# Block-sparse attention feeding an FFN: from the seventh tile on, the scores of both halves in one block and their values in another, and the fourth head in the free column group

## The chip, the cores and the metric

One core of one Trainium2 chip. The time is device microseconds of one execution of the whole program. The median over several runs is compared; the profile describes one execution.

## The reference, cut to what matters

```python
# attention: 4 batches, 8 heads, 768 tokens, head dim 64, blocks of 32 tokens (24 blocks)
scores = scale * q @ k.transpose(0, 1, 3, 2)
mask   = |qblock - kblock| <= 1, or either block is the first or the last (0, 23),
         or kblock is one of 3 blocks drawn for this qblock
attn   = exp(where(mask, scores, -1e9) - max); attn /= attn.sum(-1) + 1e-9
x      = (attn @ v).transpose(0, 2, 1, 3).reshape(3072, 512)
# FFN
h   = maximum(x @ w_in, 0)            # w_in 512 x 2048
out = (h * h) @ w_out                 # w_out 2048 x 512, all fp32
```

A query block therefore sees 8 key blocks: three of the window, the first and the last, and three drawn ones. The query blocks 0 and 23 see all 24.

## The kernel before

**Tiles and halves.** The 3072 tokens are 24 tiles of 128, listed in `order` as (b, t), batch 0 to 3 and t 0 to 5; tile number k counts from 0. A tile has four query blocks (*groups*), except t = 0 and t = 5, which have three: their first or last query block sees all keys and is done apart. Attention of a tile is done in two *halves* u of four heads each (`class Half`). Scores (`s`) go to two PSUM banks per half, by 32-column groups of TensorE, one group for each query block: window keys straight from `kn`, the keys of the whole half and batch; first, last and drawn keys from `KG`, a gathered tile. `static_keys` copies the first and last key block out of `kn` into `KG`, on ACT, for the first two tiles of each batch (there are two `KG`). DVE then takes maxima and subtracts them (`m`, `p`), ACT takes 16 small exponentials (`pm`, four for each group, 12 with three groups), DVE transposes 32 x 32 blocks (`pT`), TensorE multiplies with the values (`pv`, 65 columns a head: 64 and the sum), and DVE divides (`norm`, into `x`). Tiles 0 to 5 use another form (`exps`, `turn` by TensorE, `copies`), since `MOVED = 6`.

**Global blocks.** The query blocks 0 and 23 of a batch make four units of a head pair (`class Whole`): scores `g`, exponentials `pg`, moves `pgm`, transpose `pTg`, values `pvg`.

**FFN.** Eight chunks c of three tiles. A chunk has 16 blocks f of 128 hidden units. For each, 12 matmuls make the hidden block `ph` (line 800); ACT takes its ReLU `r` and the square `gh`; DVE takes `gf` from `ph` and `r` (line 816); POOL takes the rest `gl`; nine matmuls, two blocks later, add to the output `po` (line 838). Weights are cut in two parts on DVE and POOL (`wi`, `wo`), and in chunk 0 are also prepared by ACT from raw loads (`craw`). Chunk 0 multiplies plain fp32 (`gp`, line 828). `xt`, `xh`, `xl` turn and split x at a chunk's start; `ot` copies the output.

**The order of work** is written by hand: engines take instructions in the order of the program. The FFN of a chunk yields 96 times (*pieces*; 83 us for a chunk without global blocks, 0.86 each), and after each piece a `Stream` resumes the attention units of the chunk ahead whose time has come. A unit's own `yield n` is a lag in pieces. From chunk 2's tiles on, a half starts every 16 pieces: scores, 4 pieces, 16 exponentials with a piece between each, 11 pieces, values. So the values of a half come directly before the scores of the half two places on, in one block. The four wholes of a batch start 9 pieces behind its first four halves.

**Memory that both share.** The tag `s` has five PSUM banks, taken in turn by scores, `ph`, `pv`, `g`, `pvg`, `xt` and `pt`. The three output accumulators have their own three. Each batch's `kn` of a half is one buffer; in chunk 0 it is loaded on POOL's queue, later on SP's.

## Time and profile before

| | |
|---|---|
| median of 3 runs | 755.57 us (752.95 to 756.13) |
| profiled execution, its own time | 753.14 us |
| its span | 751.4 us |
| mean granted TensorE clock | 0.997 |
| instructions | 24184 |
| moved by DMA | 92.95 MB, 124 GB/s on the mean |

Attention of the first three tiles alone fills the first 57 us. FFN chunk 0 runs from about 57 to 153 us; from there a chunk takes 83 or 92 us, depending on whether a batch's global blocks fall into it, and the last has no attention beside it (675 to 752 us). A row of the page gives an engine's busy time; a timeline row gives a start, a length, the engine, the line, the operation with the tile written and read, and in brackets the idle time before it with what ended it. Matmul lengths overlap, so steps from start to start are what TensorE spends.

### The profile page before, as it was taken

To read this page: it belongs to the slowest core of one execution; us is meant where nothing else is said; L and a number is where in the kernel's file an instruction comes from. 1 tells how busy PE (TensorE), PEld (TensorE's weight loads), DVE (VectorE), ACT (ScalarE), POOL (GpSimd) and SP (SyncE) were. 2 spreads that over 40 slices of the span, in tenths; PEclk is the share of its full clock that TensorE was granted. 3 is DMA by queue.
4 is the path that set the end of the run, shared out by engine and by line. 5 is a ranking of instruction groups with operands and counts; after the bars stand their busy time and mean duration, and the time that the engine had idled before them with its cause. 6 is when DMAs were issued, how large, how long until landed. Compare 5 with 4: busy or idle time off the path is not lost.

```text
span 751.4 us, 24184 instructions
## 1 busy us (share of the span) xinstructions
PE 726.4 (97%) x8936; PEld 608.1 (81%) x8936; DVE 497.4 (66%) x988; ACT 518.8 (69%) x1145; POOL 500.4 (67%) x624
## 2 busy tenths in 40 slices
PE   5779999999999999999999999999999999999997
PEld 2566766678888888888888888888888888898986
DVE  5786786757786756667876665667868666545452
ACT  5997778888876866588786777578876776623222
POOL 6963643337776675767777567666867576777885
PEclk9999999999999999999999999999999999999999
DMA  8785889552533435543533435634344342101001
GB/s 276 226 231 151 261 251 344 132 156 56 144 90 92 136 85 173 150 99 101 148 72 100 132 89 177 161 85 123 93 120 102 89 129 52 34 1 43 1 1 42
DMA packets 85786, 92.95 MB, mean 124 GB/s; under 512 B 13539, under 2 KB 73060, under 8 KB 85668
## 3 DMA queue, kind: packets, MB, share of 16 engines
q1 hardware_dynamic: 79684, 68.42, 34.6%
q0 software_dynamic: 5696, 22.58, 9.2%
q8 instruction: 71, 1.16, 0.7%
q14 instruction: 47, 0.39, 0.2%
q10 hardware_dynamic: 288, 0.39, 0.1%
HBM read 85.05 MB, written 6.29 MB: 122 GB/s over the span
## 4 chain that ended last, share of the span: by engine, by line
PE 87%; ACT 6%; DVE 2%; DMA 2%; issue 1%; SPq 1%; ACTq 0%; POOL 0%; DVEq 0%; POOLq 0%
PE ph L800 34%; PE po L838 30%; PE s L373 6%; PE pv L470 6%; PE po L828 4%; PE g L558 2%; PE pvg L616 2%; DMA V<-in_v_dram 1%; PE xt L785 1%; ACT pm L418 1%; ACT V L217 1%; ACT V L209 1%; DMA kn<-in_kn_dram 1%; PE pt L447 1%; ACT p L432 1%
## 5 line engine op out<-in xcount | busy, mean ns | idle before, releaser
L800 PE MATMUL ph<-xh,wi 128*128 128x384 f32 x832 | 237.8, 346 | 0.0
L418 ACT ACTIVATE pm<-p 32x256 f32<-32x256 f32 x528 | 219.2, 415 | 15.7 <-DVE p L393 8.2
L838 PE MATMUL po<-wo,gh 128*128 128x512 f32 x672 | 213.8, 399 | 0.0
L767 POOL TENSOR_TENSOR wi<-W,wi 128x512 fp32r<-128x512 f32 x104 | 143.4, 1379 | 68.6 <-DVE wi L766 34.7
L804 ACT ACTIVATE r<-ph 128x384 f32<-128x384 f32 x128 | 63.1, 493 | 174.9 <-PE ph L800 174.0
L818 POOL TENSOR_TENSOR gl<-gf,gh 128x384 fp32r<-128x384 f32 x112 | 117.7, 1051 | 90.7 <-DVE gf L816 79.4
L767 POOL TENSOR_TENSOR wo<-WO,wo 128x512 fp32r<-128x512 f32 x112 | 146.2, 1306 | 47.4 <-DVE wo L766 46.5
L816 DVE SCALAR_TENSOR_TENSOR gf<-ph,r 128x384 f32<-128x384 f32 x112 | 62.3, 556 | 152.5 <-ACT r L804 139.9
L800 PEld LDWEIGHTS ph<-xh,wi 128*128 128x128 f32 x832 | 150.4, 188 | 13.1 <-issue 7.4
L838 PEld LDWEIGHTS po<-wo,gh 128*128 128x128 f32 x672 | 123.5, 188 | 22.8 <-issue 2.8
L800 PE MATMUL ph<-xl,wi 128*128 128x384 f32 x416 | 141.4, 340 | 0.0
L838 PE MATMUL po<-wo,gl 128*128 128x512 f32 x336 | 133.2, 397 | 0.0
L800 PEld LDWEIGHTS ph<-xl,wi 128*128 128x128 f32 x416 | 78.2, 188 | 7.0 <-issue 2.9
L766 DVE CAST wo<-WO 128x512 fp32r<-128x512 f32 x112 | 82.8, 739 | 0.0
L838 PEld LDWEIGHTS po<-wo,gl 128*128 128x128 f32 x336 | 63.1, 188 | 15.9 <-POOL gl L818 1.1
L385 DVE TENSOR_REDUCE m<-s 128x2 f32<-128x512 f32 (+1 forms) x96 | 61.5, 682 | 8.3 <-PE s L373 8.0
L811 ACT ACTIVATE gh<-r 128x384 fp32r<-128x384 f32 x112 | 59.0, 527 | 9.3 <-POOL wo L767 0.4
L470 PEld LDWEIGHTS pv<-V,pT 128*32 128x32 f32 x2816 | 46.8, 109 | 22.3 <-issue 11.0
L470 PE MATMUL pv<-V,pT 128*32 128x65 f32 x2816 | 55.1, 221 | 7.7 <-ACT pT L457 4.9
L800 PE MATMUL ph<-xh,WI 128*128 128x384 f32 x192 | 54.3, 344 | 0.8 <-ACT xh L788 0.8
L373 PE MATMUL s<-KG,q 64*32 64x160 f32 x1408 | 48.3, 301 | 0.7 <-ACT KG L288 0.7
L766 DVE CAST wi<-W 128x512 fp32r<-128x512 f32 x91 | 47.6, 523 | 0.0
(89 smaller groups left out, 918.7 us busy)
## 6 DMA issues: line engine op xcount, KB each, us to landing
craw<-in_w_dram POOLq DMA_DIRECT2D x32, 512.0 KB, 5.5
V<-in_v_dram SPq DMA_DIRECT2D x462, 32.5 KB, 1.9
KG<-in_k_dram SPq DMA_DIRECT2D x198, 64.0 KB, 1.9
V<-in_v_dram SPq DMA_DIRECT2D x28, 390.0 KB, 4.7
q<-in_q_dram SPq DMA_DIRECT2D x24, 256.0 KB, 2.8
out_dram<-ot SPq DMA_DIRECT2D x22, 256.0 KB, 3.9
V<-in_v_dram SPq DMA_DIRECT2D x16, 292.5 KB, 4.4
vn<-in_vn_dram SPq DMA_DIRECT2D x5, 780.0 KB, 5.6
```

The lines of the kernel that those rows point to most:

```text
L373: nc.tensor.matmul(self.sb[e][g * BLK : (g + 1) * BLK, i * NSLOT + a : i * NSLOT + z], q[r, j, pr, :], k, start=True, stop=True,)
L385: nc.vector.tensor_reduce(m[at, e], self.sb[e][at].rearrange("p (i c) -> p i c", i=2), axis=AX, op=ALU.max)
L418: nc.scalar.activation(p[a * BLK : (a + 1) * BLK, g], x[g * BLK : (g + 1) * BLK, :, a], AF.Exp, scale=SCALE)
L470: nc.tensor.matmul(po[g * BLK : (g + 1) * BLK, h * VW : (h + 1) * VW], self.pT[:, g, 2 * e + i, c], v[:, self.u, j, hv : hv + VW], start=( ...
L766: nc.vector.tensor_copy(w[:, 0], src)
L767: nc.gpsimd.tensor_tensor(w[:, 1], src, w[:, 0], op=ALU.subtract)
L800: nc.tensor.matmul(ph[:, :TOK], w, x, start=(i == 0), stop=(i == len(steps) - 1))
L804: nc.scalar.activation(r, ph[:, :TOK], AF.Relu)
L811: nc.scalar.activation(gh, r, AF.Square)
L816: nc.vector.scalar_tensor_tensor(gf, ph[:, :TOK], 0.0, r, op0=ALU.max, op1=ALU.mult)
L818: nc.gpsimd.tensor_tensor(gl, gf, gh, op=ALU.subtract)
L838: nc.tensor.matmul(acc[c][u], g[:, at], w[:, k], start=(f == 0 and i == 0), stop=(f == NF - 1 and i == 2))
```

## The change

From tile 6 on, two halves become a `Pair`, started every 32 pieces. Both halves' scores (four banks) are issued in one block. The maxima of half 0 follow at once, those of half 1 two pieces later. The exponentials of both halves are spread over the pieces 3 to 30, each half's transpose one piece after its last. The static keys for the next tile are copied at pieces 22 and 25. Both halves' values come in one block at piece 38, six pieces into the next pair. The first pair (tile 6, that is (1, 0)) copies the static keys of half 1 itself and then yields four pieces before its scores; those of half 0 are copied by tile 5.

In `values`, a tile with three groups used three of four column groups for each of four heads. Now the three groups of the first three heads take three column groups, and the fourth column group takes the fourth head, one group in each head's turn; `norm` then has three more small products, which put the fourth head's rows in place. This holds for all tiles.

The wholes get a table of their own for the start and for the values; their transposed tile is split in two halves that use another buffer tag.

The diff, without the parts that only carry the split of the whole's transposed tile through `copies` and `values`:

```diff
@@ -61,12 +61,17 @@
 PIECES = 96
-STEP = PIECES // (2 * UC)
+STEP = PIECES // UC
 EARLY = 23
+VALUES_AT = 38
+EXPS_AT = (3, 30)
+SECOND = 2
+KEYS_AT = 22
+BEFORE = 4
 LAST = 4
 LAG = {"s": 0, "e": 4, "v": 11, "x": 4, "t": 4, "c": 0, "v0": 13, "w0": 4, "w": 16, "n": -1}
-G_AT = 9
+WHOLES = ((9, 44), (25, 60), (41, 76), (57, 92))
 STEP_0 = 5
 STEP_1, FIRST_1 = 12, 0
@@ -335,20 +340,16 @@
             self.loads(0)
             yield lag["s"]
             self.maxima()
-            if self.moved:
-                yield lag["e"]
-                yield from self.turn_blocks()
-                yield lag["v"]
-            else:
-                yield lag["x"]
-                self.exps()
-                self.next_keys()
-                yield lag["t"]
-                pt = self.turn(bank)
-                yield lag["c"]
-                self.copies(pt)
-                self.loads(1)
-                yield lag["v0"]
+            yield lag["x"]
+            self.exps()
+            if self.u == 1:
+                self.next_keys(0)
+            yield lag["t"]
+            pt = self.turn(bank)
+            yield lag["c"]
+            self.copies(pt)
+            self.loads(1)
+            yield lag["v0"]
             po = self.values(bank)
             if lag["n"] >= 0:
                 yield lag["n"]
@@ -397,32 +398,30 @@
                     op=ALU.subtract,
                 )
-        def next_keys(self):
-
-            b, t = order[min(self.k + self.u, len(order) - 1)]
+        def next_keys(self, u):
+
+            b, t = order[min(self.k + 1, len(order) - 1)]
             if b > 0 and t < 2:
-                static_keys(b, t, 1 - self.u)
-
-        def turn_blocks(self):
+                static_keys(b, t, u)
+
+        def exps_of_blocks(self):
             x = self.p.rearrange("p h c a s -> p (h c) a s")
-            p = rot.tile([P, NJ, 8, BLK], F32, tag="p", name=f"pm{self.name}", bufs=PBUFS)
-            for g in range(NJ):
-                if g == 2:
-                    self.next_keys()
-                if g >= len(self.js):
-                    yield NJ
-                    continue
+            self.pm = rot.tile([P, NJ, 8, BLK], F32, tag="p", name=f"pm{self.name}", bufs=PBUFS)
+            for g in range(len(self.js)):
                 for a in range(NJ):
                     nc.scalar.activation(
-                        p[a * BLK : (a + 1) * BLK, g], x[g * BLK : (g + 1) * BLK, :, a], AF.Exp, scale=SCALE
+                        self.pm[a * BLK : (a + 1) * BLK, g], x[g * BLK : (g + 1) * BLK, :, a], AF.Exp, scale=SCALE
                     )
-                    yield 1
+                    yield
+
+        def turn_blocks(self):
+
+            n = len(self.js)
             self.pT = rot.tile([P, NJ, 4, 2, BLK], F32, tag="pT", name=f"pT{self.name}", bufs=2)
-            n = len(self.js)
             nc.vector.transpose(
-                self.pT[:, :n].rearrange("p j h c q -> p (j h c q)"), p[:, :n].rearrange("p j x s -> p (j x s)")
+                self.pT[:, :n].rearrange("p j h c q -> p (j h c q)"), self.pm[:, :n].rearrange("p j x s -> p (j x s)")
             )
         def exps(self):
@@ -460,35 +459,39 @@
         def values(self, bank):
             po = bank(f"pv{self.name}")
-            for i in range(2):
-                for e in range(2):
-                    h = 2 * i + e
-                    hv = h * VW
-                    for c in range(2):
-                        v = values_of(self.k)[c]
-                        for g, j in enumerate(self.js):
-                            nc.tensor.matmul(
-                                po[g * BLK : (g + 1) * BLK, h * VW : (h + 1) * VW],
-                                self.pT[:, g, 2 * e + i, c],
-                                v[:, self.u, j, hv : hv + VW],
-                                start=(c == 0),
-                                stop=(c == 1),
-                            )
+            n = len(self.js)
+            for h in range(n):
+                for c in range(2):
+                    v = values_of(self.k)[c]
+                    for g in range(NJ):
+                        src, of = (g, h) if g < n else (h, n)
+                        i, e = divmod(of, 2)
+                        j, hv = self.js[src], of * VW
+                        nc.tensor.matmul(
+                            po[g * BLK : (g + 1) * BLK, h * VW : (h + 1) * VW],
+                            self.pT[:, src, 2 * e + i, c],
+                            v[:, self.u, j, hv : hv + VW],
+                            start=(c == 0),
+                            stop=(c == 1),
+                        )
             return po
         def norm(self, po):
             t, u = self.t, self.u
             x = x_tile(self.b, t)
-            po3 = po[:, : HW // 2].rearrange("p (h c) -> p h c", h=H // 2)
+            n = len(self.js)
+            po3 = po[:, : n * VW].rearrange("p (h c) -> p h c", h=n)
             x3 = x[:, u * H // 2 * D : (u + 1) * H // 2 * D].rearrange("p (h c) -> p h c", h=H // 2)
-            rec = rot.tile([P, H // 2], F32, tag="rec", name=f"rec{self.name}", bufs=2)
-            at = self.rows
-            nc.vector.tensor_scalar(rec[at], po3[at, :, D], EPS, None, op0=ALU.add)
-            nc.vector.reciprocal(rec[at], rec[at])
-            rec3 = rec.unsqueeze(2).broadcast_to([P, H // 2, D])
-            parts = ((2 * BLK, 0, 2 * BLK), (BLK, 2 * BLK, 3 * BLK)) if t == 0 else ((0, 0, at.stop),)
+            rec = rot.tile([P, n], F32, tag="rec", name=f"rec{self.name}", bufs=2)
+            nc.vector.tensor_scalar(rec, po3[:, :, D], EPS, None, op0=ALU.add)
+            nc.vector.reciprocal(rec, rec)
+            rec3 = rec.unsqueeze(2).broadcast_to([P, n, D])
+            parts = ((2 * BLK, 0, 2 * BLK), (BLK, 2 * BLK, 3 * BLK)) if t == 0 else ((0, 0, n * BLK),)
             for to, a, z in parts:
-                nc.vector.tensor_tensor(x3[to : to + z - a], po3[a:z, :, 0:D], rec3[a:z], op=ALU.mult)
+                nc.vector.tensor_tensor(x3[to : to + z - a, :n], po3[a:z, :, 0:D], rec3[a:z], op=ALU.mult)
+            for g, j in enumerate(self.js if n < NJ else ()):
+                at = slice(n * BLK, P)
+                nc.vector.tensor_tensor(x3[j * BLK : (j + 1) * BLK, n], po3[at, g, 0:D], rec3[at, g], op=ALU.mult)
         def loads(self, step):
@@ -516,13 +519,55 @@
                 load_window(n, self.u)
                 load_sampled(n, self.u, nc.sync, SP)
+    class Pair:
+
+
+        def __init__(self, b, t):
+            self.halves = [Half(b, t, u) for u in range(2)]
+            self.b, self.t = b, t
+            self.first = order.index((b, t)) == MOVED
+
+        def events(self):
+
+            first, second = self.halves
+            ev = [(0, first.maxima), (SECOND, second.maxima)]
+            ev += [(KEYS_AT, lambda: first.next_keys(0)), (KEYS_AT + 3, lambda: first.next_keys(1))]
+            begin, end = EXPS_AT
+            n = len(first.js) * NJ
+            for h in self.halves:
+                exps = h.exps_of_blocks()
+                for i in range(n):
+                    at = begin + (i + h.u * n) * (end - begin) // (2 * n)
+                    ev.append((at, lambda exps=exps: next(exps)))
+                ev.append((at + 1, h.turn_blocks))
+            return sorted(ev, key=lambda x: x[0])
+
+        def run(self, bank, lag):
+            if self.first:
+                static_keys(self.b, self.t, 1)
+                yield BEFORE
+            for h in self.halves:
+                h.scores()
+                h.loads(0)
+            now = 0
+            for at, do in self.events():
+                if at > now:
+                    yield at - now
+                    now = at
+                do()
+            yield VALUES_AT - now
+            po = [h.values(bank) for h in self.halves]
+            for h, x in zip(self.halves, po):
+                h.norm(x)
+                h.loads(2)
+
     class Whole:
         n = (16 * BLK, 8 * BLK)
-        def __init__(self, b, pr):
-            self.b, self.pr = b, pr
+        def __init__(self, b, pr, wait=0):
+            self.b, self.pr, self.wait = b, pr, wait
             self.name = f"{b}_{pr}"
         def run(self, bank, lag):
@@ -536,7 +581,7 @@
                 yield from self.move()
                 yield lag["w0"]
                 self.turn_blocks()
-                yield lag["w"]
+                yield self.wait
             else:
                 pt = self.turn(bank)
                 yield lag["c"]
@@ -585,8 +630,12 @@
                         yield 0
         def turn_blocks(self):
-            self.pT = rot.tile([P, S], F32, tag="pT", name=f"pTg{self.name}", bufs=2)
-            nc.vector.transpose(self.pT.rearrange("p (k g q) -> p g k q", k=NT, g=NJ), self.pm)
+            self.pT = [rot.tile([P, S // 2], F32, tag="ct", name=f"pTg{self.name}_{i}", bufs=2) for i in range(2)]
+            for i in range(2):
+                nc.vector.transpose(
+                    self.pT[i].rearrange("p (k g q) -> p g k q", k=NT // 2, g=NJ),
+                    self.pm[:, :, i * NT // 2 : (i + 1) * NT // 2],
+                )
         def turn(self, bank):
             pt = [bank(f"ptg{self.name}_{i}") for i in range(2)]
@@ -640,15 +690,21 @@
     def units(c):
-        halves = [Half(b, t, u) for b, t in order[c * UC : (c + 1) * UC] for u in range(2)]
-        wholes = [] if c % 2 else [Whole(c // 2, pr) for pr in range(NPAIR)]
-        if c == 0:
-            return [(i * STEP_0, u) for i, u in enumerate(wholes + halves)]
-        if c == 1:
+        tiles = order[c * UC : (c + 1) * UC]
+        if c < 2:
+            halves = [Half(b, t, u) for b, t in tiles for u in range(2)]
+            if c == 0:
+                wholes = [Whole(0, pr) for pr in range(NPAIR)]
+                return [(i * STEP_0, u) for i, u in enumerate(wholes + halves)]
             return [(i * STEP_1 + FIRST_1, u) for i, u in enumerate(halves)]
         at = begins(c - 1) - EARLY
-        both = [(at + i * STEP, u) for i, u in enumerate(halves)]
-        both += [(at + i * STEP + G_AT, u) for i, u in enumerate(wholes)]
+        both = []
+        for i, x in enumerate(tiles):
+            u = Pair(*x)
+            both.append((at + i * STEP - (BEFORE if u.first else 0), u))
+        if c % 2 == 0:
+            turned = 1 + LAG["x"] + LAG["t"] + 2 * NJ + LAG["w0"]
+            both += [(at + x, Whole(c // 2, pr, y - x - turned)) for pr, (x, y) in enumerate(WHOLES)]
         return sorted(both, key=lambda x: x[0])
     class Stream:
```

More of the change, by code (lines that the diff above doesn't have):

```diff
@@ L599, in copies @@
         def copies(self, pt):
-            self.pT = rot.tile([P, S], F32, tag="pT", name=f"pTg{self.name}", bufs=2)
+            pT = rot.tile([P, S], F32, tag="pT", name=f"pTg{self.name}", bufs=2)
             for i, n in enumerate(self.n):
@@ L603, in copies @@
                 if i == 0:
-                    nc.scalar.copy(self.pT[:, at : at + n], pt[i][:, :n])
+                    nc.scalar.copy(pT[:, at : at + n], pt[i][:, :n])
                 else:
-                    nc.vector.tensor_copy(self.pT[:, at : at + n], pt[i][:, :n])
+                    nc.vector.tensor_copy(pT[:, at : at + n], pt[i][:, :n])
+            self.pT = [pT[:, i * S // 2 : (i + 1) * S // 2] for i in range(2)]
         def values(self, bank):
```

4 lines of the change are left out of this document (2 added, 2 removed).

## The prediction

> **What bounds the kernel now.** I read the page first: engine totals, then the chain that ended last, then the busy time by stage.
>
> ```profile
> PE 726.4 (97%) x8936; PEld 608.1 (81%) x8936; DVE 497.4 (66%) x988; ACT 518.8 (69%) x1145; POOL 500.4 (67%) x624
> ...
> PE 87%; ACT 6%; DVE 2%; DMA 2%; issue 1%; SPq 1%; ACTq 0%; POOL 0%; DVEq 0%; POOLq 0%
> ```
>
> TensorE is busy 97% of the span and 87% of the last chain is its own work. The busy times of three stages (FFN chunk 0, then two later chunks; the columns are PE, weight loads, DVE, ACT, POOL, clock, DMA share) say where:
>
> ```profile
> 57.00:153.00 96.00, 94.49 (x1127) 66.90 (x1128) 67.67 (x112) 75.98 (x151) 42.75 (x66) 1.00 0.78 225
> ...
> 245.00:328.00 83.00, 83.00 (x1023) 72.30 (x1022) 52.94 (x101) 56.77 (x129) 55.84 (x48) 1.00 0.48 131
> 328.00:420.00 92.00, 91.96 (x1201) 78.52 (x1200) 68.63 (x142) 71.81 (x167) 65.12 (x75) 1.00 0.41 105
> ```
>
> From 57 us on PE has no gaps to speak of. So an edit counts one for one in two ways only: matmul time that PE no longer spends, and waits that PE does not have today. The other engines are 60 to 80% busy and matter only where PE waits for one of them.
>
> **What the change takes off PE.** This is PE's own timeline around a half with four groups: FFN (ph), the values of an earlier half (pv), the scores of a later one (s), FFN again. Each row starts with its start and its length; records of one matmul pass are counted, two for each matmul that is written.
>
> ```profile
> 411.57 0.33 PE L800 MATMUL ph<-xl,wi 128*128 128x384 f32 x1
> 411.74 0.51 PE L800 MATMUL ph<-xh,wi 128*128 128x384 f32 x2
> 412.09 0.34 PE L800 MATMUL ph<-xl,wi 128*128 128x384 f32 x1
> 412.36 1.12 PE L470 MATMUL pv<-V,pT 128*32 128x65 f32 x64
> 413.40 0.40 PE L373 MATMUL s<-kn,q 64*32 64x96 f32 x16
> 413.59 0.48 PE L373 MATMUL s<-KG,q 64*32 64x160 f32 x16
> 413.86 0.37 PE L373 MATMUL s<-kn,q 64*32 64x96 f32 x16
> 414.03 0.58 PE L373 MATMUL s<-KG,q 64*32 64x160 f32 x16
> 414.54 0.62 PE L800 MATMUL ph<-xh,wi 128*128 128x384 f32 x2
> ```
>
> The same for a half with three groups, and a global block's pvg:
>
> ```profile
> 481.21 1.11 PE L470 MATMUL pv<-V,pT 128*32 128x65 f32 x48
> 482.25 0.38 PE L373 MATMUL s<-kn,q 64*32 64x96 f32 x12
> ...
> 482.71 0.36 PE L373 MATMUL s<-kn,q 64*32 64x96 f32 x12
> 482.88 0.48 PE L373 MATMUL s<-KG,q 64*32 64x160 f32 x12
> 483.29 0.50 PE L838 MATMUL po<-wo,gh 128*128 128x512 f32 x1
> ```
> ```profile
> 176.76 0.92 PE L616 MATMUL pvg<-vn,pTg 128*64 128x65 f32 x24
> 177.60 0.62 PE L800 MATMUL ph<-xh,wi 128*128 128x384 f32 x2
> ```
>
> Values. 64 records and 48 records both take 1.04 from start to start, so the time goes by depth: 16 steps, each four or three column groups wide. The 12 steps of pvg (two wide) take 0.84. A line through both: 0.05 a step and 0.24 for a change of block; without a fixed part it is 0.065 a step. The fourth head in the free group makes a three-group half 12 steps deep. The place is the end of tile (1,5), of three groups. On PE before (pv is the values, s the scores that follow without FFN between):
>
> ```order
> L838 MATMUL po2_0_4868<-wo2_10_5627,gl2_10_5651 128x512
> L470 MATMUL pv1_5_0_5703<-V0_78,pT1_5_0_5619 32x65 x3
> L470 MATMUL pv1_5_0_5703<-V1_79,pT1_5_0_5619 32x65 x3
> L470 MATMUL pv1_5_0_5703<-V0_78,pT1_5_0_5619 32x65 x3
> L470 MATMUL pv1_5_0_5703<-V1_79,pT1_5_0_5619 32x65 x3
> L470 MATMUL pv1_5_0_5703<-V0_78,pT1_5_0_5619 32x65 x3
> L470 MATMUL pv1_5_0_5703<-V1_79,pT1_5_0_5619 32x65 x3
> L470 MATMUL pv1_5_0_5703<-V0_78,pT1_5_0_5619 32x65 x3
> L470 MATMUL pv1_5_0_5703<-V1_79,pT1_5_0_5619 32x65 x3
> L373 MATMUL s2_0_0_0_5769<-kn2_0_5318,q2_0_5068 32x96
> ```
>
> And now:
>
> ```order
> L470 MATMUL pv1_5_0_5876<-V0_78,pT1_5_0_5612 32x65 x4
> L470 MATMUL pv1_5_0_5876<-V1_79,pT1_5_0_5612 32x65 x4
> L470 MATMUL pv1_5_0_5876<-V0_78,pT1_5_0_5612 32x65 x4
> L470 MATMUL pv1_5_0_5876<-V1_79,pT1_5_0_5612 32x65 x4
> L470 MATMUL pv1_5_1_5901<-V0_78,pT1_5_1_5709 32x65 x4
> L470 MATMUL pv1_5_1_5901<-V1_79,pT1_5_1_5709 32x65 x4
> L470 MATMUL pv1_5_1_5901<-V0_78,pT1_5_1_5709 32x65 x4
> L470 MATMUL pv1_5_1_5901<-V1_79,pT1_5_1_5709 32x65 x4
> L470 MATMUL pv1_5_1_5901<-V0_78,pT1_5_1_5709 32x65 x4
> L470 MATMUL pv1_5_1_5901<-V1_79,pT1_5_1_5709 32x65 x4
> L894 MATMUL po2_1_4901<-wo2_11_5701,gh2_11_5721 128x512 x2
> ```
>
> Eight rows three wide became six rows four wide, both halves stand together, and FFN follows. For the six pairs with three groups: 2 x 1.04 becomes 0.24 + 24 x 0.05 = 1.44, or 24 x 0.065 = 1.56; a gain of 0.52 to 0.64, I take 0.56: 3.4 in all. For the twelve pairs with four groups only a change of block goes: between the 0.09 by which the step into pv (412.09 to 412.36, 0.27) exceeds an FFN step (411.57 to 411.74, 0.17; rounded starts) and 0.24; I take 0.14, nearer the direct row: 1.7. Tile (0,5) keeps its old path but gets the new head layout: 2 x 0.2 = 0.4. Values together 5.5 (4.6 to 7.1).
>
> Scores. The first half of the block takes 0.46 (413.40 to 413.86), the second 0.68 with the change to FFN: 0.22 for that. With three groups it is 0.46 and 0.58: 0.12. Joining two halves removes one such change: at most 12 x 0.22 + 6 x 0.12 = 3.4; if issue rather than the change sets the end, a third of it. I take 2.5 (1.2 to 3.4).
>
> Entries from FFN into an attention block: 38 before, 36 after, 0.09 each: 0.2. **Taken off PE: 8.2 us (6.0 to 10.7).**
>
> **What it adds: the first pair.** Tile (1,0) is the first pair, in FFN chunk 0. Both its halves' scores now stand where only the first half's stood, so the static keys of half 1 are needed 18 us earlier. Their source kn1_1 is loaded from POOL's queue, whose order is unchanged; ACT makes the copy. ACT before, at that place (craw, W: weight preparation; p0_5_1: the exponentials of the last old half):
>
> ```order
> L722 ACTIVATE craw14_0_2251<-craw14_0_2251,below_75 128x512
> L432 ACTIVATE p0_5_1_2485<-s0_5_1_0_2448,m0_5_1_2482 96x256 x2
> L432 ACTIVATE p0_5_1_2485<-s0_5_1_1_2449,m0_5_1_2482 96x256 x2
> L288 COPY KG1_94<-kn1_0_2279 128x4x2x64
> L804 ACTIVATE r0_11_2578<-ph0_11_2495 128x384
> ```
>
> And now:
>
> ```order
> L778 ACTIVATE craw14_0_2257<-craw14_0_2257,below_75 128x512
> L293 COPY KG1_94<-kn1_1_2480 128x4x2x64
> L431 ACTIVATE p0_5_1_2491<-s0_5_1_0_2454,m0_5_1_2488 96x256 x2
> L431 ACTIVATE p0_5_1_2491<-s0_5_1_1_2455,m0_5_1_2488 96x256 x2
> L293 COPY KG1_94<-kn1_0_2285 128x4x2x64
> L860 ACTIVATE r0_11_2588<-ph0_11_2502 128x384
> ```
>
> The copy from kn1_1 moved ahead of four exponentials and of the other copy. ACT takes its work in order, so all of these wait until kn1_1 has landed. When that is, the load's issue on POOL, the answer for the tile in that window, ACT's rows and PE's two places say:
>
> ```profile
> 123.69 0.53 POOL L175 DMA_DIRECT2D kn<-in_kn_dram  x1
> ```
> ```profile
> DMA to landing us min/median/max: 10.0/10.0/10.0
> ```
> ```profile
> 127.19 1.55 ACT L432 ACTIVATE p<-s,m 96x256 f32<-96x256 f32 x4
> 128.61 0.63 ACT L288 COPY KG<-kn 128x512 f32<-128x512 f32 x1
> ```
> ```profile
> 128.50 0.38 PE L373 MATMUL s<-kn,q 64*32 64x96 f32 x12
> 129.29 0.57 PE L373 MATMUL s<-KG,q 64*32 64x160 f32 x10 [0.42 <-ACT KG L288]
> ...
> 130.36 1.98 PE L828 MATMUL po<-WO,gp 128*128 128x512 f32 x4
> ...
> 146.22 0.38 PE L373 MATMUL s<-kn,q 64*32 64x96 f32 x12
> ...
> 147.72 0.62 PE L800 MATMUL ph<-xh,wi 128*128 128x384 f32 x2
> ```
>
> kn1_1 lands at 123.69 + 10.0 = 133.7; ACT reaches the copy at 127.2 and waits 6.5. Then copy (about 0.5 as the queue moves), exponentials 1.42, copy 0.63: the keys are ready at 136.3 instead of 129.2. PE would go from kn to KG 0.19 into the block, at 128.7, and waits 7.6. Today these two blocks take 1.86 and 1.50 against 1.04 without a wait, 1.3 of waiting that goes. **Net +6.3.** Bounds: the same load at the 5.5 us that the page gives for weight loads of that queue would be +1.8; the weights that ACT prepares late may add a microsecond: 7.5.
>
> ```profile
> craw<-in_w_dram POOLq DMA_DIRECT2D x32, 512.0 KB, 5.5
> ```
>
> **The clock after such a wait.** At the start PE idled once for 2.26 us; the windows around it show the granted clock (the last figure but two):
>
> ```profile
> 19.75 1.48 PE L616 MATMUL pvg<-vn,pTg 128*64 128x65 f32 x24 [2.26 <-ACT pTg L604]
> ```
> ```profile
> 20.00:22.00 2.00, 2.00 (x28) 1.88 (x25) 0.65 (x4) 1.94 (x6) 2.00 (x5) 0.50 0.55 103
> 22.00:24.00 2.00, 2.00 (x54) 1.35 (x52) 1.29 (x5) 1.94 (x5) 1.83 (x5) 0.67 0.99 381
> ...
> 36.00:38.00 2.00, 0.55 (x29) 0.58 (x32) 1.86 (x6) 1.94 (x5) 2.00 (x8) 1.00 0.60 128
> ```
>
> Lost there: 2 x 0.50 + 2 x 0.33 = 1.7 us of full rate. The window 36 to 38, with PE idle for 1.45 of 2 us in pieces, kept 1.00. A wait of 7.6 us should cost the same **1.7** (0 to 3.4). The Trainium skill (TensorE: Matmul & The Clock Gate, Part 1) puts the fall to half rate after an idle window of about 3.4 us; this trace has it after 2.26, so for the waits of 1 to 2 us below the page gives no loss, where the row leaves one possible. That possibility is a rival below.
>
> **The second tile of chunks 1, 3 and 5.** The tag s has five PSUM banks. A hidden block ph and the four score banks of a pair take all five, so the next ph takes the bank of the one before the scores, and PE waits until DVE has read it (gf). The global blocks crowd DVE and ACT at just this tile. DVE before (pTg: a global block's transpose, ot: an output, wi, wo: weight casts):
>
> ```order
> L849 COPY ot2_1_6181<-po2_1_4869 128x512
> L766 CAST wi3_1_6189<-W11_80 128x512
> L766 CAST wo3_0_6192<-WO0_95 128x512
> L589 STREAM_TRANSPOSE pTg2_0_6200<-pgm2_0_6070 128x4x6x32
> L816 SCALAR_TENSOR_TENSOR gf3_0_6219<-ph3_0_6195,r3_0_6215 128x384
> ```
>
> And now:
>
> ```order
> L423 STREAM_TRANSPOSE pT2_0_1_6216<-pm2_0_1_6089 128x768
> L905 COPY ot2_1_6219<-po2_1_4901 128x512
> L822 CAST wi3_1_6227<-W11_80 128x512
> L822 CAST wo3_0_6230<-WO0_95 128x512
> L635 STREAM_TRANSPOSE pTg2_0_0_6238<-pgm2_0_6108 128x4x3x32
> L635 STREAM_TRANSPOSE pTg2_0_1_6239<-pgm2_0_6108 128x4x3x32
> L872 SCALAR_TENSOR_TENSOR gf3_0_6257<-ph3_0_6233,r3_0_6253 128x384
> ```
>
> The half's transpose now stands ahead of these, and a second pTg ahead of gf. What the trace of before has there:
>
> ```profile
> 337.18 0.33 PE L800 MATMUL ph<-xh,WI 128*128 128x384 f32 x1
> ...
> 338.48 0.71 PE L373 MATMUL s<-kn,q 64*32 64x96 f32 x9
> ...
> 340.00 0.44 PE L800 MATMUL ph<-xh,wi 128*128 128x384 f32 x1
> ```
> ```profile
> 340.18 0.56 DVE L816 SCALAR_TENSOR_TENSOR gf<-ph,r 128x384 f32<-128x384 f32 x1 [2.98 <-ACT r L804]
> ```
>
> gf ends at 340.74. The pair's scores would start at 337.45 and last 2 x 1.14 - 0.2, so the next ph wants the bank at about 339.6: a wait of 1.1 if DVE and ACT are as late as today. With the transposes ahead of gf it could be 2.6 (1.5 more, from 0.97 for a transpose of 768 columns and the second pTg). I take 1.95, nearer the order that will run: 3 x 1.95 = 5.9. Today the block at 338.48 lasts 1.52 instead of 1.14; such waits, three of some 0.4, go: 1.2. **Net +4.7** (2.1 to 6.6).
>
> **Costed at nothing.** The exponentials and their order on ACT: same number, spread over 27 pieces, and PE wants pT only at step 38. Three small products per three-group half on DVE and twelve split transposes: in 245 to 328 DVE has 30 of 83 us free; if that cover goes, gf comes late and PE waits, which is rival three. The value loads on SP's queue, which each half issues behind its values, come some 6 pieces later for one half and 10 earlier for the other, with the next pair's values 32 pieces away.
>
> **The sum.** -8.2 + 6.3 + 1.7 + 4.7 = +4.5. The profiled execution took 753.14, so 757.6; the median of the runs, 755.57, is 2.4 above it: **760.1**.
>
> **Rivals.** One, on the other side: kn1_1 lands before ACT asks for it. It decides at a landing within 3.5 us of the issue (123.69 to 127.2). Then neither wait nor clock is lost and today's 1.3 goes too: -8.2 - 1.3 + 4.7 = -4.8, 750.8. Against it: 10.0 measured, and a DMA share of 0.78 in this stage. Two: load at 5.5 us or clock not falling, or the bank waits at the row's 1.1: -8.2 + 1.8 + 4.7 gives 753.9 and -8.2 + 6.3 + 1.7 + 2.1 gives 757.5; around 756. Three: the clock falls at the bank waits too, 3 x 1.7, or gf is late at further tiles by as much: 765.2. Four: the joins save nothing, because issue sets the blocks' ends: without the 4.2 of joins and the 0.2, 764.5.
>
> **Chances.** Forecast 0.45, rival one 0.12, two 0.23, three 0.12, four 0.08. What a measurement of this kernel can tell from no change is about 0.5%, 3.8 us: 751.8 and 759.35. Rival one is mostly faster (0.10); two is the same, as are the quick ends of one and of the forecast (0.23 + 0.02 + 0.15): 0.40; the rest, 0.50, slower. The range reaches to between rivals one and two below and past three above: 752 to 767.
>
> **What would show it.** Right: around 128 us in the new trace, a PE wait of some 7 us released by ACT's KG copy, followed by a clock of 0.5; PE waits of 1 to 2.5 us released by DVE gf just behind the pair's scores in the second tile of three chunks; pv blocks of 1.4 to 1.6 for three groups. Wrong: no wait at 128 us (the load came early or was issued earlier), or no wait for gf, or blocks as long as two single ones.

## The result and the profile after

The changed kernel takes 764.49 us in the median (763.83 to 766.99), the kernel before 755.43 in its runs beside it: a ratio of 1.0133 (95% interval 1.0108 to 1.0159), slower. The forecast was 760.1: the sign is right, the amount is not; 4.5 us were forecast and 9.1 came. The profiled execution took 763.83 us, 10.7 more than that of before.

The page after, engine totals and the chain that ended last:

```profile
PE 726.7 (95%) x8936; PEld 613.2 (80%) x8936; DVE 506.4 (66%) x1048; ACT 517.9 (68%) x1145; POOL 496.0 (65%) x624
...
PE 76%; ACT 13%; DVE 5%; issue 2%; DMA 2%; POOL 0%; ACTq 0%; POOLq 0%; DVEq 0%
```

PE's busy time is the same as before (726.4), its share of the last chain fell from 87% to 76%. So PE gained waits, and what it saved somewhere it spent elsewhere. The largest of PE's waits from 57 us on (us in total, times, longest us):

```profile
PE s L374 <- ACT KG L293: 6.5, 1, 6.5
PE pv L470 <- issue: 1.1, 1, 1.1
PE s L374 <- ACT pg L619: 1.0, 2, 0.6
PE ph L856 <- DVE gf L872: 0.8, 3, 0.3
```

**The first pair** in PE's timeline (start, length; the block's first row, the row behind the wait, the first FFN row behind the block), the load's issue on POOL with its time to landing, and ACT's rows that PE waited for:

```profile
131.59 0.38 PE L374 MATMUL s<-kn,q 64*32 64x96 f32 x12
138.51 0.86 PE L374 MATMUL s<-KG,q 64*32 64x160 f32 x10 [6.53 <-ACT KG L293]
...
142.07 2.31 PE L884 MATMUL po<-WO,gp 128*128 128x512 f32 x4
```
```profile
127.00 0.53 POOL L180 DMA_DIRECT2D kn<-in_kn_dram  x1
```
```profile
DMA to landing us min/median/max: 8.9/8.9/8.9
```
```profile
135.88 0.62 ACT L293 COPY KG<-kn 128x512 f32<-128x512 f32 x1 [5.26 <-DMA kn<-in_kn_dram]
136.40 1.55 ACT L431 ACTIVATE p<-s,m 96x256 f32<-96x256 f32 x4
137.84 0.62 ACT L293 COPY KG<-kn 128x512 f32<-128x512 f32 x1
```

ACT waits for the load of kn1_1, then does the four exponentials, then the other copy: the order that the prediction read from the program. The block lasts 142.07 - 131.59 = 10.48 us. The granted clock (last figure but two) in and behind it:

```profile
131.00:138.00 7.00, 0.97 (x14) 0.17 (x12) 1.19 (x2) 2.12 (x6) 0.57 (x1) 0.85 1.06 298
138.00:140.00 2.00, 1.49 (x39) 1.49 (x45) 0.00 (x0) 1.97 (x5) 0.00 (x0) 0.50 0.82 172
140.00:142.00 2.00, 2.00 (x56) 1.57 (x44) 1.57 (x3) 2.00 (x4) 0.80 (x1) 0.50 0.23 52
142.00:144.00 2.00, 2.00 (x7) 1.07 (x5) 1.97 (x4) 0.34 (x1) 0.46 (x1) 0.81 0.47 103
```

The next window, from 144 on, has 1.00. Worked out from these means, the clock was at half for 2.1 + 4 + 0.8 = 6.9 us, of which 2.6 lie in the wait itself; behind the wait's end at 138.51 it was at half for 4.3.

**The second tiles**, here of chunk 3: PE's rows with a wait, DVE's rows, and the window around them:

```profile
350.25 0.68 PE L374 MATMUL s<-kn,q 64*32 64x96 f32 x9 [0.35 <-ACT pg L619]
...
352.08 0.44 PE L856 MATMUL ph<-xh,wi 128*128 128x384 f32 x1 [0.27 <-DVE gf L872]
```
```profile
348.42 0.98 DVE L423 STREAM_TRANSPOSE pT<-pm 128x768 f32<-128x768 f32 x1 [1.28 <-ACT pm L414]
...
350.55 1.03 DVE L635 STREAM_TRANSPOSE pTg<-pgm 128x384 f32<-128x384 f32 x2
351.51 0.52 DVE L872 SCALAR_TENSOR_TENSOR gf<-ph,r 128x384 f32<-128x384 f32 x1
```
```profile
348.00:352.00 4.00, 3.44 (x133) 2.33 (x131) 3.58 (x8) 3.77 (x8) 1.52 (x2) 1.00 0.46 172
```

The block takes 3.40 (348.69 to 352.08) instead of 2.08. DVE and ACT are busy 3.58 and 3.77 of 4 us; the clock stays at 1.00.

**The joined blocks.** Scores of a three-group pair, values of a four-group and of a three-group pair, each with the FFN row behind it:

```profile
290.26 0.38 PE L374 MATMUL s<-kn,q 64*32 64x96 f32 x12
...
292.18 0.44 PE L856 MATMUL ph<-xh,wi 128*128 128x384 f32 x1
```
```profile
445.19 2.36 PE L470 MATMUL pv<-V,pT 128*32 128x65 f32 x128
447.48 0.45 PE L856 MATMUL ph<-xh,wi 128*128 128x384 f32 x1
```
```profile
498.94 1.84 PE L470 MATMUL pv<-V,pT 128*32 128x65 f32 x96
500.71 0.50 PE L894 MATMUL po<-wo,gh 128*128 128x512 f32 x1
```

The scores take 1.92 where two blocks took 2.08: saved, as forecast. The values take 2.29 where two blocks took 2.09, and 1.77 where 1.44 to 1.56 was expected. Inside the block, three stretches of 0.36 us; the count behind the first busy time is PE's matmul records that touch a stretch:

```profile
445.70:446.06 0.36, 0.36 (x40) 0.36 (x32) 0.36 (x2) 0.35 (x2) 0.00 (x0) 1.00 0.49 128
446.12:446.48 0.36, 0.36 (x21) 0.36 (x10) 0.29 (x2) 0.35 (x2) 0.35 (x1) 1.00 0.55 147
446.60:446.96 0.36, 0.36 (x34) 0.36 (x33) 0.33 (x2) 0.35 (x2) 0.36 (x1) 1.00 0.49 125
```

The middle one is where the second half begins. There six records in a row start 56, 54, 56, 70, 55 and 70 ns behind their predecessor, where elsewhere four start within some 20 ns, every 57 ns. The semaphores that these six check are those that the value loads raise. But the loads were long done: SP issued the last one ahead of the block at 433.9 and it landed 1.7 us later, some 10 us before, and DVE's transpose for this half ended at 438.5. So this is not a wait for late data.

**The sum after**, from PE's starts. From the first hidden block to the last record PE takes 7.1 us longer (690.1 before, 697.2 after): the first pair's two score blocks +7.1 (10.48 for 1.86 and 1.50), the second tiles' three +2.0 (3.00, 3.40 and 3.68, for 8.1 before in all), the other joined scores -2.6, the values +1.0, FFN and its changes -0.4. The remaining 3.5 of that execution lie ahead of the first hidden block, which starts here

```profile
60.90 0.45 PE L856 MATMUL ph<-xh,WI 128*128 128x384 f32 x1 [0.67 <-ACT xh L844]
```

and at 57.35 before. Part of it is the transposes of x just ahead, here and before:

```profile
57.41 2.82 PE L841 MATMUL xt<-ident,x 128*128 128x128 f32 x12
```
```profile
55.04 1.53 PE L785 MATMUL xt<-ident,x 128*128 128x128 f32 x12
```

The granted clock was 0.60 in 57 to 59 and 0.54 in 59 to 61, and 1.00 before; 1.35 us of idle PE without a releaser stand in the values ahead of it. The runs below show this part to differ from execution to execution.

### The profile page after: what moved, and what is told of

The parts are those of the page before. It is cut to its first block, busy times and chain, and to the rows that moved or that the text cites. A ratio compares the mean times of both kernels' runs of the same rounds, so it can differ in the third digit from the quotient of the medians.

```text
span 762.0 us, 24265 instructions
## 1 busy us (share of the span) xinstructions
PE 726.7 (95%) x8936; PEld 613.2 (80%) x8936; DVE 506.4 (66%) x1048; ACT 517.9 (68%) x1145; POOL 496.0 (65%) x624
## 4 chain that ended last, share of the span: by engine, by line
PE 76%; ACT 13%; DVE 5%; issue 2%; DMA 2%; POOL 0%; ACTq 0%; POOLq 0%; DVEq 0%
PE ph L856 31%; PE po L894 29%; PE pv L470 5%; PE s L374 5%; ACT pm L414 2%; PE g L603 2%; DMA kn<-in_kn_dram 2%; ACT p L431 2%; PE pvg L666 2%; ACT craw L778 1%; PE xt L841 1%; ACT pgm L628 1%; PE po L884 1%; DVE W L787 1%; DVE m L386 1%
## 5 line engine op out<-in xcount | busy, mean ns | idle before, releaser
L823 POOL TENSOR_TENSOR wi<-W,wi 128x512 fp32r<-128x512 f32 x104 | 141.4, 1359 | 91.7 <-ACT wi L820 45.4
L822 DVE CAST wo<-WO 128x512 fp32r<-128x512 f32 x112 | 86.3, 771 | 0.3
L423 DVE STREAM_TRANSPOSE pT<-pm 128x1024 f32<-128x1024 f32 (+1 forms) x36 | 41.6, 1155 | 19.9 <-ACT pm L414 19.2
```

Source lines behind the costliest of these rows:

```text
L822: nc.vector.tensor_copy(w[:, 0], src)
L823: nc.gpsimd.tensor_tensor(w[:, 1], src, w[:, 0], op=ALU.subtract)
```

## The experiments

Each experiment's median stands beside that of the kernel before in the same job. Those without a diff of their own combine diffs already shown, or change the constant that the text names.

**The first pair alone.** Its second half goes back to its own block, 16 pieces later.

```diff
-            ev = [(0, first.maxima), (SECOND, second.maxima)]
+            late = 16 if self.first else 0
+            ev = [(0, first.maxima), (late + SECOND, second.maxima)]
+            if late:
+                ev += [(late - BEFORE, lambda: static_keys(self.b, self.t, 1))]
+                ev += [(late, second.scores), (late, lambda: second.loads(0))]
...
             if self.first:
-                static_keys(self.b, self.t, 1)
                 yield BEFORE
-            for h in self.halves:
+            for h in self.halves[: 1 if self.first else 2]:
```

> The changed kernel, but the first pair, tile (1,0), scores its second half 16 pieces later, as before the change, and copies that half's static keys 4 pieces ahead of it; everything else as in the changed kernel. Theory: the 10.5 us that TensorE spends in the first pair's block (6.5 of it one wait for ACT's KG copy, behind the load of kn1_1, the rest at a fallen clock) belongs to that one early need; it goes, the clock stays at 1.00 there, and the time falls by 6 to 8 us to about 757.5. Rival: the block only shows a backlog of ACT and of the load queue in this stage, which then shows at another place: less than 3 us, 762 or more.

755.88 us, ratio 1.0017 (0.9997 to 1.0036): 8.6 less than the changed kernel. The long wait and the slow clock are gone (0.64 us of the wait stay):

```profile
129.01 0.57 PE L374 MATMUL s<-KG,q 64*32 64x160 f32 x10 [0.64 <-ACT KG L293]
```
```profile
130.00:134.00 4.00, 4.00 (x25) 2.94 (x22) 3.82 (x6) 3.98 (x8) 1.69 (x1) 1.00 1.07 227
```

So almost the whole of the slowdown is this one early need. It does not say why the rest gained nothing.

**A piece of FFN between the two values.**

```diff
-            po = [h.values(bank) for h in self.halves]
+            po = [self.halves[0].values(bank)]
+            yield 1
+            po += [self.halves[1].values(bank)]
```

> The changed kernel with one FFN piece between the values of the two halves of a pair. In the changed kernel the joined values take 2.18 to 2.36 us (four groups) and 1.75 (three), where two single blocks took 2.09 and would take 1.64: the second half's first seven (six) matmuls stand 55 ns apart. Theory: these are the ones that carry semaphore waits, and behind FFN work such waits are passed unseen. Then each half takes 1.04 or 0.82 again, plus 0.1 for another entry: 0.1 to 0.2 us less a pair, 2 to 3 us in all, 762. Rival: the second half is slow for its own operands, wherever it stands: blocks of 1.25 and 0.95, and 0.1 more for the entry, 766.

763.59 us, 1.0119 (1.0088 to 1.0149). With the piece between, the second half of a pair looks like this:

```profile
445.28 0.51 PE L858 MATMUL ph<-xh,wi 128*128 128x384 f32 x2
445.72 1.12 PE L470 MATMUL pv<-V,pT 128*32 128x65 f32 x64
446.77 0.44 PE L858 MATMUL ph<-xl,wi 128*128 128x384 f32 x1
```

All blocks but one are 1.04 and 0.82 again, so the second half's operands are not slow in themselves. The expected gain was eaten: FFN time grew by 4.9 us with the 18 added changes between FFN and values, 0.27 each if all of it is theirs, not 0.1. The step into a block is only part of the price; the first step of FFN behind it is 0.10 longer as well (445.56 to 445.83, 0.27 instead of 0.17, in the rows of the next but one experiment). By these rows it is 0.2 each; the rest is not explained.

**The waits in the block's first quarter.** First head of both halves, then the other heads (`values` takes a bank and a slice of heads).

```diff
-            po = [h.values(bank) for h in self.halves]
+            po = [h.values(bank, heads=slice(0, 1)) for h in self.halves]
+            for h, x in zip(self.halves, po):
+                h.values(bank, x, slice(1, None))
```

> The changed kernel with the joined values issued in another order: the first head of both halves, then the other heads of the one and of the other. All matmuls that carry waits then stand in the first quarter of the block. Theory (waits that the sequencer meets in the middle of a block of short matmuls are seen, those it meets while FFN still runs are not): no run of 55 ns steps, blocks of about 1.95 (four groups) and 1.46 (three), 0.3 less a pair, 5 us in all, 759. Rival A (a block of over 64 short matmuls drains what the sequencer holds ready): the slow place stays at about half of the block, 764 to 765. Rival B (the change of PSUM bank and of the operand tiles costs it): three slow places instead of one, 0.6 more a pair, 775.

764.75 us, 1.0138 (1.0115 to 1.0162): no gain; blocks of 2.18 to 2.39, one of 4.33, and 1.75. But the slow place moved. The same view; the first stretch now begins 0.25 us into the block, behind 16 records:

```profile
445.44:445.80 0.36, 0.36 (x21) 0.36 (x11) 0.36 (x2) 0.35 (x2) 0.09 (x1) 1.00 0.58 165
446.12:446.48 0.36, 0.36 (x41) 0.36 (x34) 0.18 (x1) 0.35 (x2) 0.35 (x1) 1.00 0.46 131
```

It went from record 65 to record 17, to wherever the second half's first row stands, and there is one of it, although the block now changes bank three times. That speaks against a queue that runs dry and against the bank. It also takes away half of the theory: 16 records behind the block's start such waits still cost their time; only those of the first row cost nothing.

**Second half first.** The loads of the second half's values are issued behind the first half's on the same queues, so its waits include the other's.

```diff
-            po = [h.values(bank) for h in self.halves]
+            po = [h.values(bank) for h in self.halves[::-1]][::-1]
```

> The changed kernel with the values of a pair in the other order: second half first. Its value loads are issued behind those of the first half, so its waits on the load queues include the first half's, and the half that now stands second carries one matmul with waits instead of seven. Same matmuls, same block. Theory (each matmul that carries a wait, in the middle of a block of short matmuls, costs 55 to 70 ns instead of sharing a step of 57 with three others): blocks of 2.0 instead of 2.29 and 1.5 instead of 1.75, 5 us in all, 759.4. Rival (the first row of another half is slow for its operands and bank): no change, 764.5.

760.24 us, 1.0091 (1.0068 to 1.0114), 4.3 less than the changed kernel (3.2 by the two ratios). By the trace's records, the half that stands second now waits in its first rows only at its first matmul, for its bank. In the changed kernel nine more of its records carry a wait there (three groups: seven), and six (four) of them start alone. The blocks are

```profile
443.60 2.02 PE L470 MATMUL pv<-V,pT 128*32 128x65 f32 x128
445.56 0.44 PE L856 MATMUL ph<-xh,wi 128*128 128x384 f32 x1
445.83 0.34 PE L856 MATMUL ph<-xl,wi 128*128 128x384 f32 x1
```
```profile
496.77 1.57 PE L470 MATMUL pv<-V,pT 128*32 128x65 f32 x96
498.26 0.50 PE L894 MATMUL po<-wo,gh 128*128 128x512 f32 x1
```

1.96 and 1.50: 0.33 and 0.27 less, for six and four records that no longer start alone, some 55 to 70 ns each. With the order of matmuls, operands and banks of the same kind, that settles the seam: the waits are what cost there. But not every wait does. In the changed kernel's block at 445.19 the three records with waits right behind the six, and single ones at 445.89, 446.01 and 447.08, keep step with their neighbours. What costs is the run of six; why the others are free is not shown. Two of the twelve blocks are longer for another reason (2.28 and 4.22, see below).

**The fourth head alone**, `values` and `norm` of the change in the kernel before.

> The kernel before with one part of the change alone: the fourth head of a three-group half in the free column group, with its norm. By the changed kernel's single block of that kind (0.82 instead of 1.04) 14 halves from 57 us on save 0.22 each: 3.1 us. Theory: the first 57 us, in which the changed kernel lost 3.3, lose nothing by it, since the loss there was instruction supply of one execution: 752.4. Rival: the extra products of tile 0 on DVE (0.6 us a half, on the chain there) cause that loss: 3.3 more in the first 57 us, 755.7.

753.49 us against 754.3, 0.9983 (0.9967 to 0.9999): about 1.3 us faster. All 14 blocks are 0.82 to 0.84 instead of 1.04 (3.1 us), but FFN takes 1.1 more and the scores 0.7 more: part came back as waits. The first hidden block starts at 57.14, so the products of tile 0 do not by themselves cause the late start.

**Both edits together.**

> The changed kernel with both edits: the first pair's second half scored 16 pieces later, and the second half's values first. The two are independent by the theory: 755.9 less 5, 750.9, that is 0.995 of the kernel before. If the seam's loss moves to another wait, 755.

752.79 us against 753.17, 0.9985 (0.9963 to 1.0007). The forecast was 750.9, or 0.995: the gain is 1.9 us short by the time and 2.6 by the ratio. The profiled execution has two value blocks of 3.0 and 3.4 and a first hidden block at 59.6.

**A later start.**

```diff
-EARLY = 23
+EARLY = 20
```

> As the one before, and all attention from tile 6 on starts three pieces later (EARLY 20 for 23). The pair of the second tile then stands behind the second hidden block of a chunk with nine project matmuls (2.1 us) between it and the next hidden block, so the wait for the bank that DVE must read is covered, and ACT has three more pieces for the global block's exponentials. Theory: its three score blocks, now 3.4 to 4.2 us, come to 2.1 to 2.5: 3.5 to 5 us less, 746.5. Rival: DVE and ACT are late there because of the chunk's start, and the lateness shows at the next hidden block: 750.

749.30 us against 753.17, 0.9952 (0.9935 to 0.9968): faster than both kernels, and the best of the study. The mechanism forecast did not show: the second tiles' score blocks are still 3.55, 3.55 and 3.95 us. Two hidden blocks now stand ahead of the pair, so it is the pair that wants the bank which DVE's gf holds. The largest of that execution's waits from 58 us on:

```profile
PE s L374 <- DVE gf L875: 2.8, 3, 1.1
```

What the later start removed is the first pair's remaining wait (its block went from 2.09 to 1.08) and the wait for ACT's late pg. But the profiled executions do not show a net gain: FFN takes 2.2 us more, and from the first hidden block to the end PE needs 686.2 us against 687.2 with both edits, of which 2.5 are that one's two long value blocks. The lowest of ten runs are 748.4 and 748.1. So the 3.5 us between the two medians may be mostly such blocks, absent from this execution; that was not separated.

> The changed kernel with that later start alone. Theory: the second tile's waits (3.8 us in three blocks: 0.92, 1.32 and 1.60 over 2.08) go, the rest stays: 761. Rival as above: 764.5.

758.47 us, 1.0075 (1.0058 to 1.0092), better than the theory's number and for another reason: the three blocks are 2.57, 3.55 and 3.55, but the first pair's block halved (10.48 to 5.05), since its keys were three pieces less late: ACT waited 1.1 us for them, PE 2.8 for the copies that stand behind them on ACT, and the granted clock stayed at 1.00.

**Can the second tiles be freed?** Four tries, all on the kernel with both edits. The first moves all attention but the first pair three pieces ahead (EARLY 26), the second the second global block behind the pair (`(33, 60)` for `(25, 60)` in `WHOLES`).

> The kernel with both edits (first pair's second half later, second half's values first), and all attention from tile 6 on three pieces earlier (EARLY 26 for 23), the first pair excepted, which keeps its time. The pair of the second tile then stands ahead of the first hidden block of a chunk: its banks come from the transposes of x, which DVE has to read for that hidden block anyway, and DVE's gf of that block is wanted only four banks later. Theory (the wait is for the bank that a late gf holds): its three score blocks come from 3.4 to 4.2 us to 2.1 to 2.6, 3 to 5 less than with both edits alone (752.8), 748.5. Rival: DVE is late with everything at a chunk's start, and the scores or the next hidden block wait as long for it there: 752.

> The kernel with both edits, and the second global block of a batch scored at piece 33, behind the second tile's pair, instead of 25, ahead of it. Then its maxima, its two exponentials of 0.69 and 0.47 us and its bank are out of the way of that pair and of gf. Theory (the global block makes ACT and DVE late there): the wait for ACT's pg (0.5 us in each of three blocks) goes and gf comes about 1 us earlier: blocks of 2.1 to 2.5, 3 to 5 us less than 752.8. Rival (the chunk's own start, xh, xl and the output's copies, makes them late): only the wait for pg goes, 1.5 us.

768.23 us (1.0195, 1.0168 to 1.0221) and 766.28 (1.0174, 1.0139 to 1.0210): both are clear misses. With the early start the score blocks did shrink to 2.1 to 2.3, and the wait went to the transposes of x, 2.8 us in each of two chunks, with 6.7 us of waits for wi from POOL and DVE beside it:

```profile
336.16 0.77 PE L844 MATMUL xt<-ident,x 128*128 128x128 f32 x4 [2.80 <-DVE gf L875]
```

With the global block later, the hidden block waits for gf longer than before, then the global block's scores for the pair's maxima, and DVE is busy in all of those 7 us:

```profile
348.61 0.44 PE L859 MATMUL ph<-xh,wi 128*128 128x384 f32 x1 [1.92 <-DVE gf L875]
350.50 1.53 PE L606 MATMUL g<-kn,QG 128*128 128x512 f32 x4 [0.93 <-DVE p L394]
```
```profile
345.00:352.00 7.00, 4.15 (x121) 3.01 (x105) 7.00 (x14) 1.93 (x4) 4.06 (x4) 1.00 0.48 164
```

Both kernels also lost clock at these waits. With the early start it was at half for 3.4 us from 336.6, right behind the wait shown above, though not behind its like at 515.2. With the global block later it was at half for 3.4 us from 170.4, behind waits of 1.60 and 1.79, and for 6.8 us from 525.4, behind one of 1.96. That is up to 1.7 and 5.1 us of full rate.

The other two split the second tile's scores, two banks at a time, with either start:

```diff
-            late = 16 if self.first else 0
+            late = 16 if self.first else 6 if self.t == 1 else 0
```

> The kernel with both edits and the start three pieces later (EARLY 20; 749.3 us), in which also the second tile of each batch scores its two halves six pieces apart, two banks at a time instead of four. Theory (four banks taken at once next to one or two hidden blocks leave the next user with a bank that a late DVE still has to read; two do not): each of the three places, blocks of 3.55 to 3.95, becomes 1.14 behind FFN and 1.14 behind the values, less than 0.3 of waits: 1.2 less a place, 3 to 4 in all, 746. Rival (whatever takes banks there waits for the late gf): 749.5.

> The same split of the second tile's scores on the kernel with both edits and the old start (EARLY 23; 752.8 us). Theory: blocks of 3.4, 3.4 and 4.16 become 1.14 (up to 0.6 more where ACT's pg is late) and 1.14: 3 us less, 749.5. Rival: 752.8.

756.43 us (1.0021, 1.0008 to 1.0035) and 753.38 (0.9993, 0.9973 to 1.0012). With the start at 20 it is worse than unsplit, the wait for gf stays and others for DVE come:

```profile
344.47 0.31 PE L374 MATMUL s<-kn,q 64*32 64x96 f32 x7 [1.13 <-DVE gf L876]
357.29 0.45 PE L860 MATMUL ph<-xh,wi 128*128 128x384 f32 x1 [1.03 <-DVE x L494]
```

With the start at 23 the blocks shrink (1.77, 1.77 and 2.25, then 1.14), but the hidden blocks next to them wait for wi from POOL and DVE, 0.8 and 0.6 us at a time, and nothing is left. In these places DVE is the bound for some us; freeing a bank there moved the wait and did not remove it.

## Why the prediction was right or wrong

**What bounds it.** Right from 57 us on: every us there is matmul time that PE lost or saved, some of it at half clock, or a wait that it had not had. The first 57 us were put at nothing, and the profiled execution lost 3.5 us there.

**The first pair and the clock.** Right in place, releaser and size. +6.3 and +1.7 were forecast; the two blocks took 7.1 us more, half-rate records included, and taking the early need away returned 8.6 in the medians. ACT waited 5.3 us at the copy rather than 6.5, since the load landed in 8.9 us rather than 10.0. The granted clock cost 3.5 x 0.5 + 2 x 0.19 = 2.1 us of full rate behind the wait; 1.7 were forecast. Rival three in its first form, a fall of the clock at the bank waits, did not come: they were under 1 us here, and the clock stayed at 1.00. At longer ones it was real, as the runs with the early start and the later global block show. The Trainium skill (TensorE: Matmul & The Clock Gate, Part 1) puts the fall after at least one idle window of about 3.4 us. These runs had it after waits of 1.96 and 2.80 us, and kept 1.00 after others of 2.8, so here the length alone does not decide.

**The second tiles.** Right in mechanism, too large: net +2.6 with the joins set apart (3.8 of waits for 1.2 of today), forecast +4.7. DVE's order was as read, the two pTg, the casts and pT ahead of gf, with DVE waiting 1.28 us for the last exponential. But in two of the three places the pair's scores waited 0.35 and 0.6 us for ACT's pg in the same stretch, and gf ran at the same time: what was left behind it was 0.3 us a place.

**Scores and entries.** Forecast -2.5 and -0.2, measured -2.6 in fourteen pairs (-3.2 with the second tiles) and -0.4.

**The values: the step that failed.** "For the twelve pairs with four groups only a change of block goes". It was forecast as -1.7 for these, -3.4 for three groups and -0.4 for tile (0,5), 5.5 in all; it came as +3.5 (1.3 of it one block of 3.52 us), -2.1 and -0.4: +1.0. This term of the sum, off by 6.5 us, is more than the whole miss. The working took a joined block as its matmuls plus one change less. It left out that a half's first row carries waits for its loads, which stand behind FFN in every pv block of before from tile 6 on and cost nothing seen there, and which the join puts in the middle of the block. The run with the second half first shows it: 0.33 and 0.27 us back a pair, 12 x 0.33 + 6 x 0.27 = 5.6. Then four groups give 2.09 - 1.96 = 0.13 a pair and three groups 2.08 - 1.50 = 0.58: the 0.14 and 0.56 of the working. So the terms of the sum were right for matmuls without such waits; the step that failed is that nothing else comes with the join.

The measured 764.5 is the number of rival four. That is chance: its reason, joins that save nothing because issue sets the ends, is wrong for the scores, which saved what was forecast, and for the values the join cost time.

Put together: 4.5 forecast, plus 6.5 for the values, less 0.9 for the first pair and the clock, 2.1 for the second tiles and 0.9 for scores and entries is the 7.1 of PE's time.

**What stays open.** The profiled executions reach the first hidden block between 57.1 and 60.9 us: at 57.1 to 57.4 in two kernels with the old order of tiles from 6 on, and in twelve with the new order five times there and seven times at 59.0 to 60.9, though what stands ahead of it hardly differs from the run with the fourth head alone. In six of these seven, and in none of the others, the clock was at half for 3.4 us somewhere between 50 and 61 us; what comes first there is open. Likewise in seven of the twelve one or two joined or second value blocks, nine in all, are 1.1 to 2.3 us longer, with a hole of 0.8 to 2.0 us in which PE waits for nothing that the profile shows (1.1 in the changed kernel's list above). In all nine a transfer on the profile's instruction queue q8 starts between 0.4 us ahead of the block's start and 1.6 behind it; many blocks with such a transfer have no hole, so a late supply of instructions fits but is not shown. Whether the new order brings these on or an execution has them by chance was not separated; the 2 us by which the medians differ more than PE's sum may be of these two.

## What to carry to other kernels

A block of short matmuls is not the sum of its matmuls when it is joined from parts: look for a run of instructions with waits that the join moves from behind long work into the middle, and order the parts so that the one with the latest loads comes first and its waits cover the others'. When two needs are brought together, look for the later of the two supplies on every in-order queue in between; here one 0.6 us copy on ACT, standing behind a load, held PE for 6.5 us. A burst that takes nearly all banks of a rotation makes the slowest reader of the one left the bound, and moving the burst moves the wait.

## What the hardware showed

In a run of waits in the midst of short matmuls, each one starts 54 to 70 ns behind its predecessor, though the data had landed some 10 us before, where four without waits share a step of 57. In the first row of a block behind FFN the same waits cost nothing, and neither do single ones in the middle. A change from FFN to such a block and back costs FFN 0.2 us by its steps, 0.09 into the block and 0.10 at the first step behind it, beside the 0.15 from the block's last matmul to the first of FFN (447.33 to 447.48 in the changed kernel). After 6.5 us of idle PE the granted clock was 0.50 for 4.3 us more; it fell also after waits of 1.96 and 2.80 us, and did not after others of 2.8. Its falls lasted about 3.4 us, or two or three times that.
